# Opening order of TensorE's work, and the place of the w1 stage in the first and last block of a fused attention and MLP kernel

## The chip, the core and the metric

The kernel runs on one core of one Trainium2 chip. The metric is the device time of one execution in microseconds (us), as the median over several runs. The hardware profiler gives one more execution, with a trace of every instruction on TensorE (PE for products, PEld for weight loads), the vector engine (DVE), the scalar engine (ACT), GpSimd (POOL) and SyncE (SP), and of the DMA queues.

## What is computed

The input x has 2048 rows (tokens) of 576 columns. In outline, all in bfloat16:

```python
xn = layernorm(x)
# A: attention over the last W = 512 keys of a cache; 32 query heads, 16 key heads, head size 128
q  = xn @ wq                                  # 576 -> 32 * 128
p  = softmax(q @ k.T * 128 ** -0.5)           # no mask
s  = (p @ v) @ wo                             # 4096 -> 576
# B: a token-shift block and an MLP, on the same xn
h  = gelu(layernorm(xn) @ w1)                 # 576 -> 576
hs = (quarters of h shifted by +1, -1, +2, -2 rows) @ w2
x1 = xn + hs
b  = x1 + gelu(layernorm(x1) @ w3) @ w4       # 576 -> 4608 -> 576
out = x + s * silu(b)
```

## The kernel before

**Tiling.** The rows are cut into NB = 4 blocks of QB = 512, each of TB = 4 tiles of 128 rows. The first phase runs over blocks, and in each over the Hq = 32 heads. A step is one head of one block; its number is u = 32 * block + head, so there are 128 steps. The second phase (the MLP with w3 and w4, and the final combination) follows, block by block.

**One step of the first phase.** `stage_s(u, i)` makes four score tiles with keys as weights (L363), each followed by an exponential on ACT (L365). `stage_q(u + 1)` makes the next head's q with five 512-column products (L348). Its copy qT out of PSUM runs on the vector engine in block 0 (L353) and on ACT later (L355). `stage_v(u - 1, .)` makes the previous head's output in two halves of eight products (L380). The vector engine divides by the softmax sum (L384, L385) and writes a tile `o` from a ring of four buffers. `stage_t(u - 1)` sends a DMA transpose of `o` into `oT` on SP's queue (L393).

**Work put between.** Two dictionaries hold other work by step: `fill` (called once, after the next q) and `pe_fill` (lists of single products, cut in three and laid between the score tiles). The helpers `at`, `pe`, `spread` and `later` fill them. For each block they hold:
- `ln2_steps`: the LayerNorm for the w1 stage, at heads 7 to 9, and `tr2`: four DMA transposes on SP (L312) into `xnnT`, at heads 10 to 13
- `b1`: the w1 stage, five groups of five products (L452) on `xnnT`, with a GELU chain `gelu1_` on the vector engine and ACT after each group (L467 to L475), at heads 15 to 19
- `b2_shift`, `b2` and `b2_rem`: the w2 stage (L503) of the previous block, at heads 21 to 24, and in the last block also that of the last block itself, at heads 26 to 29; `b2_rem` ends with a 576 KB write of x1 to DRAM on SP's queue (L530)
- `wo_atoms`: the output product of the previous block, at heads 1 to 5
- `load_x` for the next block, `ln1_steps` (its LayerNorm, at heads 20 to 22 in block 0 and 24 to 26 in blocks 1 and 2) and `tr1` (its DMA transposes on SP's queue, L312, into `xT_b`, at heads 23 to 26 in block 0)
- `prep_k` (L247): four transposes on TensorE for one key head, with a copy out of PSUM, at the odd steps of block 0 up to 27

At the end of the last block come `load_x1(0)` at head 10, `ln3_steps(0)` from head 25 and `ln3_transpose(0)` at head 29 for the second phase.

**What sets the order.** `tc.manual_schedule(engines={SP, POOL, PE})` makes SP, POOL and TensorE run the first phase in the written order. The vector engine and ACT are ordered by a list scheduler, in which `tc.high_priority(offset=HP)` puts a section ahead of later work: the copies qT and kT, the division by the softmax sum, the GELU chain and the w2 additions have it, the LayerNorms don't. Each engine runs its list in order.

**Buffers.** The PSUM tiles are three for scores (tag `sc`), two shared by q, w1 and the remainder of w2 (`pq`), two for head outputs (`po`) and one (`wo`) shared by key transposes, wo and w2.

**The opening.** `ln1_steps(0)` is emitted first. TensorE then runs 32 small products of the identity with itself into `wu`, the key transposes of heads 0 and 1, four 512-column products of the identity with raw x, the 20 transposes of `tr1_first` (L319) into five PSUM tiles that ACT and the vector engine copy to `xT_b`, and the first q.

Of the kernel before, what the change touches and what calls it, by code (L numbers as in the profile page):

```python
# [8 lines left out]
P = 128  # L9
# [20 lines left out]
def kernel(  # L30
# [14 lines left out]
    nc = tc.nc  # L45
# [3 lines left out]
    _, S, D = A_x.shape  # L49
    _, Hkv, Sk, Dh = A_k_cache.shape  # L50
# [9 lines left out]
    QB = 512  # L60
    NB = S // QB
# [21 lines left out]
    ident = const.tile([P, P], BF16, name="ident")  # L83
# [88 lines left out]
    with ExitStack() as actx:  # L172
# [33 lines left out]
        x_t = {}  # L206
# [33 lines left out]
        def prep_k(g):  # L240
            st = {}
            src = kst_t[g // 4][:].rearrange("p a b -> p (a b)")[:, (g % 4) * W:(g % 4 + 1) * W]

            def tr(kc):
                if kc == 0:
                    st["ps"] = ps_wo.tile([P, W], BF16, name="ps_k", tag="wo")
                nc.tensor.transpose(out=st["ps"][:, kc * P:(kc + 1) * P], in_=src[:, kc * P:(kc + 1) * P],  # L247
                                    identity=ident[:, :])
                if kc == KCH - 1:
                    if g < 2:  # L250
                        nc.scalar.activation(out=kT[:, g, :], in_=st["ps"][:, :], func=ACT.Copy)
                        return
                    with tc.high_priority(offset=HP):
                        nc.vector.tensor_copy(out=kT[:, g, :], in_=st["ps"][:, :])

            return [lambda kc=kc: tr(kc) for kc in range(KCH)]

        def late(ap, fn):
            g = nc.gpsimd.tensor_copy(out=gate[:, :], in_=ap)
            with tc.issue_after(g.ins):  # L260
                fn()
# [44 lines left out]
        def ln1_steps(b):  # L306
            xn_t[b] = xn_b[b % 2]
            return layernorm_steps(small, [xn_b[b % 2][:, tt, 0:D] for tt in range(TB)], [x[:] for x in x_t.pop(b)],
                                   rsqrt_newton if b else rsqrt_table)
# [32 lines left out]
        def stage_q(u):  # L342
            qb, h = divmod(u, Hq)
            w = wq_b[(u // 4) % NWQ]
            hh = h % 4
            psq = ps_pq.tile([P, QB], FP32, name="psq", tag="pq")
            for kc in range(NDC):
                nc.tensor.matmul(psq[:, :], lhsT=w[:, kc, hh * Dh:(hh + 1) * Dh], rhs=xT_b[qb % 2][:, kc, :],  # L348
                                 start=(kc == 0), stop=(kc == NDC - 1))
            qT = qT_pool.tile([P, QB], BF16, name="qT")  # L350
            with tc.high_priority(offset=HP):
                if qb == 0:
                    nc.vector.tensor_copy(out=qT[:, :], in_=psq[:, :])  # L353
                else:
                    nc.scalar.activation(out=qT[:, :], in_=psq[:, :], func=ACT.Copy)  # L355
            qT_t[u] = qT
# [76 lines left out]
        def ln2_steps(b):  # L433
            return layernorm_steps(small, [xnn_b[:, tt, 0:D] for tt in range(TB)],
                                   [xn_t[b][:, tt, 0:D] for tt in range(TB)])

        def tr2(b, tt):
            transpose_tile(xnnT, xnn_b, tt)

        def b1(b, c):  # L440
            st = {}

            def mm(kc):
                if kc == 0:
                    if c == 0:
                        hb_t[b] = hb_pool.tile([P, 5, QB + 2 * PAD], BF16, name="hb")
                        if b == 0:
                            nc.vector.memset(hb_t[b][:, :, 0:PAD], 0.0)
                        if b == NB - 1:
                            nc.vector.memset(hb_t[b][:, :, PAD + QB:], 0.0)  # L450
                    st["ph"] = ps_pq.tile([P, QB], FP32, name="ph", tag="pq")
                nc.tensor.matmul(st["ph"][:, :], rhs=xnnT[:, kc, :],  # L452
                                 lhsT=w1r_sb[:, kc, :] if c == 4 else w1_sb[:, kc, c * c4:c * c4 + P],
                                 start=(kc == 0), stop=(kc == NDC - 1))
                if kc == NDC - 1:
                    gelu1(b, c, st["ph"])

            return [lambda kc=kc: mm(kc) for kc in range(NDC)]

        def gelu1(b, c, ph):  # L460
            with tc.high_priority(offset=HP):
                gelu1_(b, c, ph)
# [21 lines left out]
        def b2_shift(b):  # L484
            with tc.high_priority(offset=HP):
                b2_shift_(b)
# [67 lines left out]
        def at(u, fn):  # L554
            fill.setdefault(u, []).append(fn)

        def pe(u, atoms):
            pe_fill.setdefault(u, []).extend(atoms)
# [5 lines left out]
        def later(u, make, per):  # L564
            cell = []
            for i in range(2 * TB + 1):
                def step(i=i):
                    if not cell:
                        cell.append(make())
                    cell[0][i]()  # L570
                at(u + i // per, step)

        for b in range(NB):
            base = b * Hq
            if b > 0:
                for i, group in enumerate(wo_atoms(b - 1)):
                    pe(base + 1 + i, group)
            later(base + 7, lambda b=b: ln2_steps(b), 3)
            for tt in range(TB):
                at(base + 10 + tt, lambda b=b, tt=tt: tr2(b, tt))  # L580
            for c in range(5):
                pe(base + 15 + c, b1(b, c))
            for bb in ([b - 1] if b > 0 else []) + ([b] if b == NB - 1 else []):
                o2 = base + (26 if bb == b else 21)
                at(o2 - 1, lambda bb=bb: b2_shift(bb))
                for tt in range(TB):
                    pe(o2 + tt, b2(bb, tt))
                pe(o2 + 3, b2_rem(bb))
            if b + 1 < NB:
                at(base + (8 if b == 0 else 4), lambda b=b: late(pT_t[b * Hq + (8 if b == 0 else 4)][0][0:1, 0:1],  # L590
                                                                 lambda: load_x(b + 1, nc.gpsimd)))
                u1 = base + (24 if b else 20)
                later(u1, lambda b=b: ln1_steps(b + 1), 3)
                for tt in range(TB):
                    at(u1 + (3 + tt // 2 if b else 3 + tt), lambda b=b, tt=tt: tr1(b + 1, tt))
# [24 lines left out]
        at(3 * Hq + 4, finish_flag)  # L620

        with tc.manual_schedule(engines={SP, POOL, PE}):
            x_raw = x_t[0][0]
            for step in ln1_steps(0):
                step()
            wu = ps_sc.tile([P, QB], FP32, name="warm", tag="sc")
            for i in range(32):
                nc.tensor.matmul(wu[:, 0:P], lhsT=ident[:, :], rhs=ident[:, :], start=True, stop=True)
            for g in range(2):
                for fn in prep_k(g):  # L630
                    fn()
            for i in range(4):
                nc.tensor.matmul(wu[:, :], lhsT=ident[:, :], rhs=x_raw[:, 0:QB], start=True, stop=True)
            tr1_first()
            stage_q(0)
            for u in range(0, max(max(fill), max(pe_fill)) + 1):
                atoms = pe_fill.get(u, []) + [fn for v, g in pe_late if v == u for fn in prep_k(g)]
                n = len(atoms)
                cut = [atoms[0:n // 3], atoms[n // 3:2 * n // 3], atoms[2 * n // 3:]]
                for i in range(4):  # L640
                    if u < U:
                        stage_s(u, i)
                    if i == 0:
                        if u + 1 < U:
                            stage_q(u + 1)
                        for fn in fill.get(u, []):
                            fn()
                        continue
                    if i < 3 and 0 <= u - 1 < U:
                        stage_v(u - 1, 2 * (i - 1))  # L650
                    for fn in cut[i - 1]:
                        fn()
                if 0 <= u - 1 < U:
                    stage_t(u - 1)


    with ExitStack() as bctx:
# [90 lines left out]
        for b in range(NB):  # L748
# [20 lines left out]
            else:  # L769
# [9 lines left out]
                for i in range(3):  # L779
                    lo, hi = cuts[i], cuts[i + 1]  # L780
                    ps = pm[TB - 1 - i][:, 0:hi - lo]
                    for fc in range(FC):
                        nc.tensor.matmul(ps, lhsT=h3_t[fc][:, tt * P:(tt + 1) * P],
                                         rhs=w4_s[fc // WS][:, fc % WS, lo:hi], start=(fc == 0), stop=(fc == FC - 1))
# [4 lines left out]
    with tc.If(flag > 0):  # L789
        with ExitStack() as gctx:  # L790
# [19 lines left out]
            with tc.For_i(0, NT, 1) as t:  # L810
# [10 lines left out]
                for h in range(Hq):  # L821
                    g = h // REP
# [14 lines left out]
                    for kc in range(NDC):  # L837
                        nc.tensor.matmul(pq[:], lhsT=wq_sb[:, kc, h * Dh:(h + 1) * Dh], rhs=xnT[:, kc, :],
                                         start=(kc == 0), stop=(kc == NDC - 1))
# [19 lines left out]
                    for kc in range(KCH):  # L859
                        nc.tensor.matmul(po[:], lhsT=v_g[:, kc, :], rhs=pT[:, kc * P:(kc + 1) * P],  # L860
                                         start=(kc == 0), stop=(kc == KCH - 1))
# [5 lines left out]
                for ps, lo, hi in ((pm, 0, M0), (pr, M0, D)):  # L867
                    for h in range(Hq):
                        nc.tensor.matmul(ps[:], lhsT=oTs[h][:], rhs=wo_sb[:, h, lo:hi], start=(h == 0),
                                         stop=(h == Hq - 1))  # L870
# [39 lines left out]
```

## Time and profile before

| quantity | value |
|---|---|
| median of 12 runs | 870.26 us (865.8 to 882.49) |
| profiled execution | 867.96 us, of which the span in the trace is 865.9 us |
| TensorE products busy | 846.1 us (98% of the span) |
| ACT busy | 457.2 us (53%) |
| vector engine busy | 390.6 us (45%) |
| first score product starts | 16.07 us |
| last head output ends, first last-block wo product starts | 530.51 us |
| second phase, first w3 product starts | 561.9 us |

Times in the trace count from the start of the span. In lines of the trace, the first number is the start, the second the duration of the group, then engine, line, operation, tiles and shapes, and in brackets how long the engine had been idle and what released it. In lists of waits the three numbers are the total, how many times, and the longest. Matmuls are pipelined and their ends are modelled, so starts are the better numbers; the share of busy time is an average over stages.

### The profile page before, as it was taken

How to read it: one execution, taken by the hardware profiler on the slowest of the kernel's cores; microseconds unless marked ns; L12 is line 12 of the kernel's file. 1: busy time of each engine (PE TensorE's matmuls, PEld its weight loads, DVE VectorE, ACT ScalarE, POOL GpSimd, SP SyncE). 2: the span in 40 equal slices, each digit the busy share in tenths (PEclk: the TensorE clock that was granted, in tenths of full speed). 3: DMA queues.
4: the chain of work that ended last, by engine and by line, in shares of the span. 5: the costliest groups of instructions: out<-in, count | busy, mean ns of one | idle time of the engine just before them, and what ended most of it. 6: DMA issues, size and time to landing. Idle time of an engine off the chain costs nothing.

```text
span 865.9 us, 16302 instructions
## 1 busy us (share of the span) xinstructions
PE 846.1 (98%) x6512; PEld 472.6 (55%) x6512; DVE 390.6 (45%) x1210; ACT 457.2 (53%) x819; POOL 80.7 (9%) x143
## 2 busy tenths in 40 slices
PE   6989999999999999999999999999999999999996
PEld 4655655665665565565565565544444444444455
DVE  4778941278861287881155775000053026005024
ACT  4766763498783398784377873133242233225510
POOL 2432200310010110111010102000000000000000
PEclk9999999999999999999999999999999999999999
DMA  6995781374361184374147438990023005001001
GB/s 167 201 262 135 155 115 44 103 129 93 87 134 40 41 146 76 91 149 61 13 101 141 92 59 197 320 258 1 1 72 96 1 8 159 3 1 56 0 15 45
DMA packets 138098, 83.74 MB, mean 97 GB/s; under 512 B 104496, under 2 KB 131376, under 8 KB 138016
## 3 DMA queue, kind: packets, MB, share of 16 engines
q1 hardware_dynamic: 126448, 51.24, 30.1%
q0 software_dynamic: 8448, 28.15, 11.4%
q10 hardware_dynamic: 3120, 3.25, 1.1%
q8 instruction: 53, 0.87, 0.4%
q14 instruction: 29, 0.24, 0.1%
HBM read 49.17 MB, written 9.44 MB: 68 GB/s over the span
## 4 chain that ended last, share of the span: by engine, by line


## 5 line engine op out<-in xcount | busy, mean ns | idle before, releaser
L365 ACT ACTIVATE pT<-sc 128x512 bf16<-128x512 f32 x512 | 289.0, 596 | 107.0 <-PE sc L363 100.0
L363 PE MATMUL sc<-qT,kT 128*128 128x512 bf16 x512 | 182.6, 378 | 1.0 <-DVE qT L353 0.8
L705 PE MATMUL ph<-xT_b,w_s 128*128 128x512 bf16 x720 | 172.1, 379 | 0.0
L708 ACT ACTIVATE h<-ph 128x512 bf16<-128x512 f32 x144 | 85.6, 596 | 155.6 <-PE ph L705 151.0
L380 PEld LDWEIGHTS <-pT 128*128 128x128 bf16 x2048 | 139.2, 98 | 52.3 <-DVE o L385 1.8
L380 PE MATMUL po<-v_sb,pT 128*128 128x129 bf16 x2048 | 162.0, 220 | 0.4 <-ACT pT L365 0.4
L348 PE MATMUL psq<-xT_b,wq_b 128*128 128x512 bf16 x640 | 159.0, 379 | 0.5 <-DVE xT_b L325 0.3
L714 PE MATMUL pm<-w_s,h 128*128 128x512 bf16 x540 | 145.8, 380 | 0.0
L728 DVE TENSOR_TENSOR bs<-pm,x 128x512 f32<-128x512 f32 (+3 forms) x18 | 11.1, 629 | 246.3 <-PE pm L714 198.4
L404 PE MATMUL pswo<-wo_sb,oT 128*128 128x512 bf16 x512 | 116.5, 379 | 0.0
L384 DVE RECIPROCAL ri<-po 128x2 f32<-128x2 f32 x256 | 42.5, 166 | 162.6 <-PE po L380 159.4
L385 DVE TENSOR_TENSOR o<-po,ri 128x256 bf16<-128x256 f32 x256 | 107.6, 420 | 9.3 <-DMA oT<-o 3.1
L705 PEld LDWEIGHTS <-w_s 128*128 128x128 bf16 x720 | 63.8, 98 | 73.4
L348 PEld LDWEIGHTS <-wq_b 128*128 128x128 bf16 x640 | 62.4, 98 | 74.5 <-issue 2.4
L715 PE MATMUL pr<-w_s,h 128*128 128x64 bf16 x540 | 99.1, 193 | 0.0
L404 PEld LDWEIGHTS <-oT 128*128 128x128 bf16 x1024 | 64.9, 98 | 55.2
L714 PEld LDWEIGHTS <-h 128*128 128x128 bf16 x540 | 52.7, 98 | 63.8 <-issue 0.6
L355 ACT ACTIVATE qT<-psq 128x512 bf16<-128x512 f32 x96 | 57.4, 598 | 27.9 <-PE psq L348 27.9
L363 PEld LDWEIGHTS <-kT 128*128 128x128 bf16 x512 | 47.5, 97 | 29.4 <-DVE qT L353 1.3
L715 PEld LDWEIGHTS <-h 128*128 128x128 bf16 x540 | 51.0, 98 | 12.2 <-issue 0.4
L220 POOL DMA_DIRECT2D wq_b<-in_A_wq_dram x30 | 23.3, 778 | 310.3 <-PE psq L348 237.7
L414 ACT ACTIVATE s_out<-pswo 128x512 bf16<-128x512 f32 x16 | 9.6, 597 | 48.2 <-PE pswo L404 48.2
(101 smaller groups left out, 509.6 us busy)
## 6 DMA issues: line engine op xcount, KB each, us to landing
wq_b<-in_A_wq_dram POOLq DMA_DIRECT2D x30, 512.0 KB, 5.4
w_s<-in_B_w_dram SPq DMA_DIRECT2D x9, 576.0 KB, 8.8
wo_sb<-in_A_wo_dram POOLq DMA_DIRECT2D x8, 576.0 KB, 5.0
w_s<-in_B_w_dram SPq DMA_DIRECT2D x9, 512.0 KB, 9.5
x_dram<-x SPq DMA_DIRECT2D x4, 576.0 KB, 4.1
x<-x_dram SPq DMA_DIRECT2D x4, 576.0 KB, 4.5
s_b<-s_dram SPq DMA_DIRECT2D x4, 576.0 KB, 6.4
x_b<-in_A_x_dram SPq DMA_DIRECT2D x4, 576.0 KB, 6.1
```

What stands on the lines that cost most here:

```text
L348: nc.tensor.matmul(psq[:, :], lhsT=w[:, kc, hh * Dh:(hh + 1) * Dh], rhs=xT_b[qb % 2][:, kc, :], start=(kc == 0), stop=(kc == NDC - 1))
L355: nc.scalar.activation(out=qT[:, :], in_=psq[:, :], func=ACT.Copy)
L363: nc.tensor.matmul(sc[:, :], lhsT=kT[:, g, kc * P:(kc + 1) * P], rhs=qT_t[u][:, :], start=True, stop=True)
L365: nc.scalar.activation(out=pT[:, :], in_=sc[:, :], func=ACT.Exp, scale=SCALE)
L380: nc.tensor.matmul(po[:, j, :], lhsT=pTs[kc][:, tt * P:(tt + 1) * P], rhs=v_sb[:, g, kc, 0:Dh + 1], start=(kc == 0), stop=(kc == KCH - 1))
L384: nc.vector.reciprocal(out=ri[:], in_=po[:, :, Dh])
L385: nc.vector.tensor_tensor(out=o[:, t0:t0 + 2, :], in0=po[:, :, 0:Dh], in1=ri[:].unsqueeze(2).to_broadcast([P, 2, Dh]), op=ALU.mult)
L404: nc.tensor.matmul(ps, lhsT=oT_t[qb * Hq + h][:, tt, :], rhs=wo_sb[:, h, lo:hi], start=(h == 0), stop=(h == Hq - 1))
L705: nc.tensor.matmul(ph[:, :], lhsT=w3[:, kc, f0:f0 + P], rhs=xT_b[b % 2][:, kc, :], start=(kc == 0), stop=(kc == NDC - 1))
L708: nc.scalar.activation(out=h3[:, :], in_=ph[:, :], func=ACT.Gelu_apprx_tanh)
L714: nc.tensor.matmul(pm[tt][:, :], lhsT=lhsT, rhs=w4[:, fc % WS, 0:M0], start=(fc == 0), stop=(fc == FC - 1))
L715: nc.tensor.matmul(pr[:, tt, :], lhsT=lhsT, rhs=w4[:, fc % WS, M0:D], start=(fc == 0 and tt == 0), stop=(fc == FC - 1), skip_group_check=True)
```

## The change

In the opening, the 32 identity products become 36. The key transposes of head 0 follow, then 28 more identity products in place of the four 512-column ones, then `tr1_first` and the first q. The second key head's transposes move behind the first q. In blocks 0 and 3, the w1 stage goes from heads 15 to 19 to heads 17 to 21. In block 3 the w2 stage of block 2 goes from heads 21 to 24 to heads 23 to 26, and that of block 3 from heads 26 to 29 to heads 28 to 31. `b2_shift` moves along with each. Everything else is emitted at the steps where it was.

```diff
             for c in range(5):
-                pe(base + 15 + c, b1(b, c))
+                pe(base + (15 if 0 < b < NB - 1 else 17) + c, b1(b, c))
             for bb in ([b - 1] if b > 0 else []) + ([b] if b == NB - 1 else []):
-                o2 = base + (26 if bb == b else 21)
+                o2 = base + (28 if bb == b else 23 if b == NB - 1 else 21)
                 at(o2 - 1, lambda bb=bb: b2_shift(bb))
...
         with tc.manual_schedule(engines={SP, POOL, PE}):
-            x_raw = x_t[0][0]
             for step in ln1_steps(0):
                 step()
             wu = ps_sc.tile([P, QB], FP32, name="warm", tag="sc")
-            for i in range(32):
-                nc.tensor.matmul(wu[:, 0:P], lhsT=ident[:, :], rhs=ident[:, :], start=True, stop=True)
-            for g in range(2):
-                for fn in prep_k(g):
-                    fn()
-            for i in range(4):
-                nc.tensor.matmul(wu[:, :], lhsT=ident[:, :], rhs=x_raw[:, 0:QB], start=True, stop=True)
+
+            def warm(n):
+                for _ in range(n):
+                    nc.tensor.matmul(wu[:, 0:P], lhsT=ident[:, :], rhs=ident[:, :], start=True, stop=True)
+
+            warm(36)
+            for fn in prep_k(0):
+                fn()
+            warm(28)
             tr1_first()
             stage_q(0)
+            for fn in prep_k(1):
+                fn()
             for u in range(0, max(max(fill), max(pe_fill)) + 1):
```

## The prediction

> **What bounds the kernel now.** I read the page first: engine shares, then the list of TensorE's waits, then the timeline of the opening, of the two places where the w1 stage begins, and of what the vector engine and SP do after the first of them.
>
> ```profile
> PE 846.1 (98%) x6512; PEld 472.6 (55%) x6512; DVE 390.6 (45%) x1210; ACT 457.2 (53%) x819; POOL 80.7 (9%) x143
> ```
>
> TensorE's sequence sets the end; a microsecond in which it stands still is a microsecond of the total, unless a later wait gives it back. Its waits (in total, times, longest):
>
> ```profile
> PE ph L452 <- DMA xnnT<-xnn_b: 3.3, 2, 2.8
> PE ps_k L247 <- ACT kT L251: 2.6, 1, 2.6
> ...
> PE ps_k L247 <- DMA x<-in_A_k_cache_dram: 1.6, 1, 1.6
> PE ph L452 <- issue: 1.6, 1, 1.6
> ```
>
> All four are in what the change touches. The opening, on TensorE (start, duration, then idle before and releaser):
>
> ```profile
> 6.74 0.61 PE L247 MATMUL ps_k<-ident,x 128*128 128x128 bf16 x4 [1.56 <-DMA x<-in_A_k_cache_dram]
> 9.98 0.58 PE L247 MATMUL ps_k<-ident,x 128*128 128x128 bf16 x4 [2.64 <-ACT kT L251]
> 10.36 1.91 PE L633 MATMUL warm<-xt,ident 128*128 128x512 bf16 x4
> 12.07 1.63 PE L319 MATMUL ps_x<-ident,xn_b 128*128 128x128 bf16 x20
> 13.99 1.30 PE L348 MATMUL psq<-xT_b,wq_b 128*128 128x512 bf16 x5 [0.29 <-DVE xT_b L325]
> 16.07 0.38 PE L363 MATMUL sc<-qT,kT 128*128 128x512 bf16 x1 [0.78 <-DVE qT L353]
> ```
>
> The normalised x tile is complete at 8.18 + 1.45 = 9.63 us (vector engine, L139), but its transposes start at 12.07: the second head's keys wait 2.64 us for their one PSUM tile, then four 512-column products go first. The two w1 starts, in blocks 0 and 3:
>
> ```profile
> 65.17 0.81 PE L452 MATMUL ph<-xnnT,w_sb 128*128 128x512 bf16 x3 [2.75 <-DMA xnnT<-xnn_b]
> ...
> 467.56 0.38 PE L452 MATMUL ph<-xnnT,w_sb 128*128 128x512 bf16 x1 [1.56 <-issue]
> ```
>
> After block 0's w1 stage, the vector engine:
>
> ```profile
> 107.30 0.42 DVE L385 TENSOR_TENSOR o<-po,ri 128x256 bf16<-128x256 f32 x1
> ...
> 112.12 0.42 DVE L385 TENSOR_TENSOR o<-po,ri 128x256 bf16<-128x256 f32 x1 [1.76 <-DMA oT<-o]
> ```
>
> and SP's queue there:
>
> ```profile
> 101.10 1.21 SPq L312 DMA_TRANSPOSE xT_b<-xn_b  x1
> 102.36 1.26 SPq L393 DMA_TRANSPOSE oT<-o  x1
> 103.72 1.25 SPq L312 DMA_TRANSPOSE xT_b<-xn_b  x1
> 105.02 1.38 SPq L393 DMA_TRANSPOSE oT<-o  x1
> ```
>
> Outputs of later heads already wait here for transposes that stand behind those of block 1's x.
>
> **What the skill says.** "TensorE: Matmul & The Clock Gate", section "What's actually happening": the array runs at half clock until a window of about 3.4 us was busy, and the window is free-running, so the switch moves from run to run. The trace agrees on two rates: the four 512-column products from 10.36 to 12.07 are 0.43 us apart, those of a later q 0.216. Full speed appears only inside the 20 transposes after 12.07; the 3.6 us of small products from 1.59 did not bring it. The same page, section "Part 4: PE-mode transpose", holds that transposes do not count as busy in the same way; this trace cannot tell, since products and transposes share the window before the switch. "DMA: Bandwidth & Descriptors", section "Queues, rings and completion order": on each DMA engine descriptors of a queue are taken in ring order. The trace fits: the x transpose issued at 103.72 lands after 8.1 us, and the oT transpose behind it after 7.0, against a median of 3.5.
>
> **Opening.** Removed: four 512-column products (1.71 us, 10.36 to 12.07). Added: 4 + 28 small products. Moved: four key transposes of the second head, behind the first q. The first group rises to 36 x 0.107 = 3.9 us, ends at 5.4 and still waits for keys landing at 6.74: free. Keys of the first head to 7.2; then 28 x 0.107 = 3.0 us at half clock, to 10.2 (1.6 us at full clock). Then tr1_first, its data ready at 9.63. At half clock its 20 transposes take 2.1 us to 12.3 and the PSUM copies begin at 12.45 instead of 13.51: **-1.1 us**. If the clock switches by about 9.4 (the product stream is unbroken from 6.74), small products end at 9.8, the transposes take 1.2, and copies begin at 11.1: **-2.4**. If transposes do not count and the switch comes only after 16, q, scores and values run at half speed for some 6 us, +1 to +2. Weights do not stop it: wq's first pair, issued at 2.70 and 3.21, landed at 9.4 and 9.6. The moved key transposes (4 x 0.056 to 0.107) fit in the 0.78 us wait for the first qT, their copy on ACT before the first exponential; without that cover 0.4 us. I take -1.3, with -2.4 and +1.5 as ends. Nothing limits it later: TensorE is the bound right after.
>
> **Block 0.** A head takes 2.88 us on TensorE, 3.10 with key transposes, 1.08 more with five w1 products. Head 15 takes 7.09 instead of 4.18: 2.9 us. Two heads later, the w1 products start at about 67.5, while xnnT landed at 65.1: that wait goes. No product is added. But the 5 GELU chains (7 vector operations each, some 2.1 us of spacing) move with it from heads 15-19 to 17-21 and now overlap heads 20-22, in which block 1's LayerNorm is queued. From 67.4 to 104.2 the vector engine is busy 35.3 of 36.8 us: saturated. LayerNorm has the lower priority; when TensorE is a head ahead, one more head of vector work is in front (1.7 us by spacing: qT 0.6, twice a reciprocal 0.12 and a product 0.34, keys 0.33 every other head). So its first apply (100.65 now) does not come earlier, and I put it 0 to 4 us later. What waits for it: SP issues block 1's first x transpose (fixed in order at head 23), behind it stands the oT transpose of head 22, and head 26's output needs that buffer of a ring of four. Today it lands at 102.36 + 4.8 = 107.2, the output is at 107.30: **no margin**. TensorE itself bears about 1.5 us of this (the 1.76 us wait at 112.12 lengthened its head from 2.88 to only 3.08). So with the apply unmoved, 2.9 - 1.5 = 1.4 us is given back, leaving 1.5; for each microsecond that apply is later, one more goes. In its favour: the 576 KB wo and 512 KB wq loads (issued 101.68 and 103.60, five to seven us each), which crowd these transposes, now run some 3 us before them. I take **-1.2** net; ends -2.9 (nothing given back) and +2.5 (apply 4 us later).
>
> **Block 3.** Head 15: 5.68 instead of 3.96, 1.7 us, goes likewise (xnnT is there before 467.6; the stage now begins near 471). There is no next LayerNorm of x here and qT is copied on ACT, so the vector engine has room: 25.7 of 35.2 us busy. The w2 groups of blocks 2 and 3 move two heads as well; the last now fills heads 28 to 31. That covers the end of attention, where exponentials lag: a 0.35 us wait at 529.74 and 0.2 us in the product before. Another 0.4: **-2.1**. What moves with it on SP: the 576 KB write of x1 (L530) now stands just before the last two oT transposes. They are issued at about 1.6 us after attention's end, as today (531.13 and 532.4 against 530.51), landing 4.0 later; the wo products first need them 30 x 0.216 = 6.5 us after. Margin under 1 us: ends -2.4 and +2. LayerNorm for the MLP shares heads with the w2 additions; its result is needed at 561.9 and its transposes go out at 520.5, so it has room.
>
> **Sum.** -1.3 - 1.2 - 2.1 = -4.6 us. The profiled execution was 867.96 us (span 865.9 and 2.1 around it), so it would be 863.4. The median of the runs shown is 870.26, 2.3 above; with the same step, **865.7 us**. 0.5% is 4.35 us, about what a measurement here can tell from no change; my sum stands just beyond it.
>
> **Rivals.** (1) *Everything is kept*: the crowding is gone, outputs do not wait, the clock is up early: -2.4 - 2.9 - 2.1 = -7.4, 862.9 us. For it: four plain waits in the list; against: the margin of zero at 107.3. (2) *Block 0 gives all back*: saturated vector engine, apply 2 us later, opening at half clock: -1.1 + 0.5 - 2.1 = -2.7, 867.6 us. For it: 35.3 of 36.8. (3) *Slower: the SP queue in block 0 becomes the bound.* Apply 4 us later, and head 22's oT transpose takes 8.4 us instead of 4.8, as its neighbours did (8.1, 7.0): output of head 26 is 7.6 us late against today, plus 0.3 through what follows. From 4.9 us on (1.5 of margin, 1.3 and 2.1 elsewhere) it decides: -4.9 + 7.9 = +3.0, 873.3 us. (4) *The change misses its place*: if waits are set by something else that moves along (xnnT later because SP is busy), both w1 starts wait again and only the opening counts: 869 us; SP's issue of xnnT is ahead of the moved part, so I give this little.
>
> **How the numbers follow.** My forecast 0.46, (1) 0.20, (2) with (4) 0.22, (3) 0.12. The forecast's own range is 863.5 to 868, a little over half of it beyond 4.35 us. Faster by over 0.5%: 0.28 + 0.20 = 0.48; slower by over 0.5%, only the far part of (3) and an opening left at half clock: 0.10; within: 0.42. The range of 8 in 10 takes in (1), (2) and the near part of (3): 862.0 to 871.3.
>
> **What would show it.** Right: first score product at 13.7 to 15.0 instead of 16.07; no wait on xnnT; block 0 with an o<-oT wait of 2 us or more around head 26; attention's end with no 0.35 us wait. Wrong: transposes and first q at 0.43 us a product until beyond 16; block 1's first apply no later in heads than now; TensorE waiting for oT after attention.

## The result and the profile after

The changed kernel takes 865.28 us in the median of 12 runs (861.05 to 884.96), against 872.12 us for the kernel before (49 runs in all): a ratio of 0.9924, with an interval of 0.9897 to 0.9952. In a later set of runs it was 0.9918 (0.9887 to 0.9950). The forecast was 865.7. The profiled execution took 865.29 us, of which the span is 863.5. Some executions of any version are disturbed and left out of the ratios; two profiles below (of `e2_b0` and `f4_after_wo_ln1`) were of that kind and are not read.

The engines' shares, and TensorE's two longest waits from its list (in total, times, longest):

```profile
PE 848.5 (98%) x6540; PEld 475.6 (55%) x6540; DVE 390.6 (45%) x1210; ACT 457.6 (53%) x819; POOL 80.8 (9%) x143
```

```profile
PE po L380 <- DVE o L385: 2.1, 1, 2.1
PE psq L348 <- DMA xT_b<-xn_b: 2.0, 1, 2.0
```

The waits before the w1 stages of blocks 0 and 3 and both on keys have gone from the top. (Before, the list put the 1.56 us of block 3 down to "issue", but the last transpose into `xnnT` landed at 467.47 there and the products began at 467.56: it was a wait for `xnnT` too.) Two others stand there instead: head outputs that wait for the vector engine, and block 3's first q that waits for its transposed x. The opening on TensorE:

```profile
1.59 4.02 PE L629 MATMUL warm<-ident 128*128 128x128 bf16 x36 [1.59 <-POOL ident masks.py:199]
5.92 0.61 PE L247 MATMUL ps_k<-ident,x 128*128 128x128 bf16 x4 [0.31 <-DMA x<-in_A_k_cache_dram]
6.32 1.96 PE L629 MATMUL warm<-ident 128*128 128x128 bf16 x28
8.62 1.47 PE L319 MATMUL ps_x<-ident,xn_b 128*128 128x128 bf16 x20 [0.34 <-DVE xn_b L139]
10.38 1.31 PE L348 MATMUL psq<-xT_b,wq_b 128*128 128x512 bf16 x5 [0.29 <-DVE xT_b L325]
11.53 0.39 PE L247 MATMUL ps_k<-ident,x 128*128 128x128 bf16 x4
12.47 0.38 PE L363 MATMUL sc<-qT,kT 128*128 128x512 bf16 x1 [0.56 <-DVE qT L353]
```

The 28 products take 1.96 us, not 28 x 0.107 = 3.0: the clock rose inside them, for at 6.8 us the spacing of their starts goes from 0.107 to 0.056 us. Scores start at 12.47, not 16.07. The first w1 products of block 0 and of block 3, in the same timeline:

```profile
65.96 0.59 PE L452 MATMUL ph<-xnnT,w_sb 128*128 128x512 bf16 x2
...
471.25 0.38 PE L452 MATMUL ph<-xnnT,w_sb 128*128 128x512 bf16 x1
```

No bracket stands at their ends: no wait. Then the vector engine, where block 1's LayerNorm and the outputs meet:

```profile
97.94 0.43 DVE L139 TENSOR_SCALAR xn_b<-xt,ln_mv,nr_y 128x576 bf16<-128x576 bf16 x1
...
100.63 0.16 DVE L384 RECIPROCAL ri<-po 128x2 f32<-128x2 f32 x1
104.68 0.42 DVE L385 TENSOR_TENSOR o<-po,ri 128x256 bf16<-128x256 f32 x1 [3.89 <-DMA oT<-o]
```

SP's queue, with the output transposes queued between those of block 1's x:

```profile
98.40 1.20 SPq L312 DMA_TRANSPOSE xT_b<-xn_b  x1
99.65 1.32 SPq L393 DMA_TRANSPOSE oT<-o  x1
101.06 1.23 SPq L312 DMA_TRANSPOSE xT_b<-xn_b  x1
102.34 1.87 SPq L393 DMA_TRANSPOSE oT<-o  x1
```

The oT transpose issued at 99.65 lands 4.9 us later, at 104.59, and the vector engine, which needs that buffer for its next `o`, resumes at 104.68. TensorE there and at block 3's start, and the granted clock (columns: stretch, length, TensorE busy with its instructions, clock, share of the DMA engines, GB/s):

```profile
105.16 0.64 PE L380 MATMUL po<-v_sb,pT 128*128 128x129 bf16 x8 [2.12 <-DVE o L385]
...
107.64 2.02 PE L348 MATMUL psq<-xT_b,wq_b 128*128 128x512 bf16 x5
...
384.70 1.38 PE L348 MATMUL psq<-xT_b,wq_b 128*128 128x512 bf16 x5 [2.02 <-DMA xT_b<-xn_b]
```

```profile
103.00:105.00 2.00, 0.04 (x1) 1.00 0.72 149
105.00:107.00 2.00, 1.84 (x18) 0.70 0.49 94
107.00:109.00 2.00, 2.00 (x6) 0.50 0.69 135
...
386.00:388.00 2.00, 2.00 (x15) 0.50 1.13 139
```

After each of these waits the clock drops to half for about 3.4 us, which costs another 1.7: from about 105.8 to 109.2 and from 385.7 to 389.1 the products start at half the rate. The "busy" column hides it: the engine is at 2.00 of 2.00 while a q takes 2.02 us instead of 1.24.

The difference of the two profiled executions by stage, from the starts of products. Block 0 is counted from the second q, which starts right after the first score, the other blocks from their own first q:

| stage | before | after | difference | forecast |
|---|---|---|---|---|
| start to first score | 16.07 | 12.47 | -3.60 | -1.3 |
| block 0 | 100.89 | 101.48 | +0.59 | -1.2 |
| block 1 | 133.76 | 133.76 | 0 | 0 |
| block 2 | 135.73 | 136.77 | +1.04 | 0 |
| block 3, to its first wo product | 143.84 | 143.26 | -0.58 | -2.1 |
| second phase, to the last product | 328.38 | 328.38 | 0 | 0 |
| sum | | | -2.55 | -4.6 |

The medians are 6.8 us apart, more than the two profiles (2.67 us). The profiled execution of before, at 867.96, was a quick one among 49 with a median of 872.12; that of after is at its median. So more than half of the gain in the medians (4.2 of 6.8 us) is a difference that no pair of traces shows. One part of it may be the old opening: in e3 and f1 below, which have it, scores started at 16.70 and 17.35, later than the 16.07 of before.

### The profile page after: what moved, and what is told of

It is laid out like the page before. It is cut to its first block, busy times and chain, and to the rows that moved or that the text cites. A ratio compares the mean times of both kernels' runs of the same rounds, so it can differ in the third digit from the quotient of the medians.

```text
span 863.5 us, 16356 instructions
## 1 busy us (share of the span) xinstructions
PE 848.5 (98%) x6540; PEld 475.6 (55%) x6540; DVE 390.6 (45%) x1210; ACT 457.6 (53%) x819; POOL 80.8 (9%) x143
## 4 chain that ended last, share of the span: by engine, by line
```

## The experiments

Accounts to tell apart: (a) the parts need each other, since `xnnT` arrives late in block 0 however early TensorE gets there, and an earlier opening only lengthens that wait unless the w1 stage moves too; (b) the parts add up, each with its own gain; (c) the opening alone is the gain. Beside that: what of block 0's gain comes back at the ring of `o`.

The runs came in four sets, each with its own runs of before: the change; e1 to e4; f0 to f4; g1, e6, g3 and g4. Only the first and the third hold the change itself, so the other ratios are compared with it across sets. The stages are those of the table above, in us. The traces of e1, e3 and e4 lack some matmul records, so their stages are good to about 0.2 us.

| kernel | ratio, interval | first score | block 0 | block 2 | block 3 |
|---|---|---|---|---|---|
| before | 1 | 16.07 | 100.89 | 135.73 | 143.84 |
| the change | 0.9924 (0.9897-0.9952) | 12.47 | 101.48 | 136.77 | 143.26 |
| e1_open | 1.0029 (1.0001-1.0056) | 16.14 | 110.13 | 136.76 | 143.18 |
| e2_b0 | 0.9964 (0.9933-0.9994) | - | - | - | - |
| e3_b3 | 1.0019 (0.9980-1.0058) | 16.70 | 101.93 | 135.22 | 141.85 |
| e4_open_b3 | 0.9995 (0.9966-1.0025) | 12.52 | 107.76 | 137.26 | 141.85 |
| f0_after, the change again | 0.9918 (0.9887-0.9950) | 16.02 | 101.99 | 140.87 | 141.63 |
| f1_before_wo | 0.9937 (0.9910-0.9965) | 17.35 | 99.73 | 136.16 | 143.03 |
| f2_after_wo | 0.9881 (0.9836-0.9926) | 12.68 | 99.41 | 136.36 | 141.63 |
| f4_after_wo_ln1 | 0.9879 (0.9830-0.9929) | - | - | - | - |
| g1_keys_last | 0.9916 (0.9877-0.9955) | 12.89 | 99.50 | 140.72 | 141.64 |
| e6_ln1early | 0.9901 (0.9864-0.9937) | 13.62 | 97.26 | 137.74 | 141.63 |
| g3_open_b3_wo | 0.9918 (0.9884-0.9952) | 14.17 | 97.63 | 137.30 | 141.64 |
| g4_best | 0.9912 (0.9883-0.9941) | 12.98 | 104.33 | 136.21 | 141.63 |

Block 1 took 133.75 to 134.48 us in every one of these profiles.

### The parts by themselves

The opening alone, on the kernel before, with `warm` as in the change:

```diff
...
-            for g in range(2):
-                for fn in prep_k(g):
-                    fn()
-            for i in range(4):
-                nc.tensor.matmul(wu[:, :], lhsT=ident[:, :], rhs=x_raw[:, 0:QB], start=True, stop=True)
...
+            warm(36)
+            for fn in prep_k(0):
+                fn()
+            warm(28)
             tr1_first()
             stage_q(0)
+            for fn in prep_k(1):
+                fn()
```

> The opening alone, both w1 and w2 stages as before. Theory (opening and block 3 carry the gain, block 0 gives all back): -3.6 us by the profile after (first score product at 12.5 instead of 16.1), in the median -2.5 to -4. Rival (block 0 carries 2.9 in most runs and the profiled execution of after was an unlucky one): opening only -1.5 to -2.5. In the profile: half clock gone before 8 us, q(32) 3.6 earlier than before, the two waits on xnnT (2.75 and 1.56 us) still there.

Measured: 1.0029, no gain, so that neither of the two expectations held. From the list of TensorE's waits, and the timeline of the opening and of the w1 start:

```profile
PE ph L452 <- DMA xnnT<-xnn_b: 9.7, 1, 9.7
```

```profile
8.18 0.61 PE L247 MATMUL ps_k<-ident,x 128*128 128x128 bf16 x4 [2.57 <-DMA x<-in_A_k_cache_dram]
8.58 3.19 PE L629 MATMUL warm<-ident 128*128 128x128 bf16 x28
11.57 2.27 PE L319 MATMUL ps_x<-ident,xn_b 128*128 128x128 bf16 x20
...
72.15 1.44 PE L452 MATMUL ph<-xnnT,w_sb 128*128 128x512 bf16 x3 [9.66 <-DMA xnnT<-xnn_b]
```

Two things differ from the profile of the whole change. TensorE could go on with the keys only at 8.18, after it had stood still for 2.57 us, and all 28 products and the 20 transposes ran at half clock: scores started at 16.14, as before. And in block 0 the last transpose into `xnnT` took 12.1 us to land, so TensorE waited 9.66.

Block 0 alone, and block 3 alone:

```diff
-                pe(base + 15 + c, b1(b, c))
+                pe(base + (17 if b == 0 else 15) + c, b1(b, c))
```

> Only the w1 stage of block 0 two heads later; opening, block 3 as before. Theory: the 2.75 us wait goes and comes back as a wait of head outputs on the oT transposes around head 27, perhaps with half clock after it: -0.5 to +1.0 us. Rival: -2.5 us or more, no such wait over 1 us on TensorE.

```diff
-                pe(base + 15 + c, b1(b, c))
+                pe(base + (17 if b == NB - 1 else 15) + c, b1(b, c))
...
-                o2 = base + (26 if bb == b else 21)
+                o2 = base + (28 if bb == b else 23 if b == NB - 1 else 21)
```

> Only block 3: w1 two heads later, w2 stages two heads later. Both theories: -1.7 to -2.1 us, the 1.56 us wait gone and nothing in its place. If the write of x1 now ahead of the last oT transposes costs: a wait of the wo products after attention, 0 or slower.

Measured: block 0 alone 0.9964, a gain of 0.4% whose interval nearly touches 1. That is some 3 us (0.5 to 5.8), nearer the rival's size than the theory's; whether a wait of head outputs came in is not shown. Block 3 alone cannot be told from no change in the runs, but its stage in the profile is 141.85 against 143.84 us: -2.0. It is 141.6 to 141.9 in each profile of a kernel with this part except that of the change itself, where the half clock after 384.70 runs into it. Without this part the stage took 143.0 to 143.2 us in e1 and f1, where TensorE waited before w1 for 0.7 and 0.8 us and not for 1.56: there the part would save some 1.4 us. In e3 block 0's wait is the old one, 2.45 us, this time with the half clock behind it.

The opening and block 3 together, w1 in block 0 left where it was (the edit is against the changed kernel):

```diff
-                pe(base + (15 if 0 < b < NB - 1 else 17) + c, b1(b, c))
+                pe(base + (17 if b == NB - 1 else 15) + c, b1(b, c))
```

> Opening and block 3, block 0 as before. Theory: as fast as the whole change (-5 to -6.5 us against before). Rival: 2 to 3 us slower than the whole change (-3.5 to -4.5 us against before), since block 0's part is missing.

Measured: 0.9995, so that both expectations failed here too. The opening took its early course (scores at 12.52) and block 3 was 2 us shorter, yet nothing is left of it:

```profile
65.74 1.44 PE L452 MATMUL ph<-xnnT,w_sb 128*128 128x512 bf16 x3 [6.88 <-DMA xnnT<-xnn_b]
```

The w1 stage starts at 65.74; before the change it was 65.17. Everything the opening had gained was waited away there: the last transpose into `xnnT` landed at 65.6, as late as before (65.0), though it had been issued 2.8 us earlier. It isn't so in every execution. In the profile of the change it landed at 62.1, and w1 at its old place would have waited about 3.4 us by my estimate (2.75, less 3.0 for the landing, plus 3.6 for the opening). The parts do not add up: +0.3%, -0.4% and +0.2% alone, -0.05% for two of them, -0.8% for all three.

### What makes xnnT late

Eight loads of `wo`, 576 KB each, are issued at heads 4, 7, ... 25 of block 0, on GpSimd's queue. They move here to heads 16 to 23, behind the `xnnT` transposes, once in the kernel before and once in the changed one; the change is repeated beside them.

```diff
-            at(4 + 3 * i, lambda i=i: late(pT_t[4 + 3 * i][0][0:1, 0:1], lambda: load_wo(i)))
+            at(16 + i, lambda i=i: late(pT_t[16 + i][0][0:1, 0:1], lambda: load_wo(i)))
```

> The whole change again, beside the next three. Theory now (the parts need each other: the last transpose of xnnT in block 0 lands 7 to 18 us after its issue, set by bulk loads and not by TensorE's pace, so an earlier opening only lengthens the wait there unless w1 is later): -0.5 to -0.9% against before, as measured. Rival (the first comparison was luck and the parts' 0 to -0.4% add up): -0.2 to -0.4%.

> The kernel before, only the eight wo loads of block 0 moved from heads 4, 7, ... 25 to heads 16 to 23. Theory (wo loads crowd the xnnT transposes): last xnnT lands within 5 us of its issue instead of 7, TensorE's 2.75 us wait on it shrinks to under 1 us, median -2.5 to -5 us against before and fewer slow executions. Rival (landing is slow by the transposes themselves, or by wq, v and x loads): wait and median unchanged within 1 us.

> The whole change with the wo loads at heads 16 to 23. Theory: xnnT is there long before head 17 in every execution; what is left is the wait of head outputs on oT behind block 1's x transposes near head 27, which the earlier end of the wo loads shortens: 1 to 3 us faster than the whole change. Rival: the loads now crowd heads 20 to 27 and the output wait grows: equal or 1 to 3 us slower than the whole change.

Measured: the kernel before gains 0.6% from this alone (0.9937), and the changed one goes to 0.9881. On the same chip `f2` has a median of 862.6 us in six runs and the change 866.0: 3.4 us less (2.3 to 6.3 when the runs are resampled), so f2 beats both kernels. Of the four `xnnT` transposes of block 0, the time from issue to landing in the kernel before and then in f1:

```profile
DMA to landing us min/median/max: 4.4/5.5/6.9
```

```profile
DMA to landing us min/median/max: 2.8/3.9/5.5
```

In f1 block 0 no longer waits for `xnnT`; the loads' price is a wait for wq, which they now delay:

```profile
PE psq L348 <- DMA wq_b<-in_A_wq_dram: 2.1, 1, 2.1
PE ph L452 <- DMA xnnT<-xnn_b: 0.9, 1, 0.9
```

The 0.9 is at 331.37, in block 2. The same move in e4, the kernel in which block 0's w1 stage is not shifted:

> The opening and block 3 as in the change, block 0's w1 stage where it was before, and the eight loads of wo moved to heads 16 to 23 of block 0. Without that move of the loads the same kernel measured 0.9995. Theory (block 0's shift of w1 is worth only the margin that it gives against the crowding of the transposes by the loads of wo; with the crowding gone the margin is worth nothing): as fast as the whole change with moved loads, 0.987 to 0.989, with no wait for xnnT in block 0. Rival (the w1 stage itself is better placed two heads later, or the earlier opening runs into the transposes in any case): 0.991 to 0.996, with a wait for xnnT of 1 us or more near 65 us.

In the profile it did what was expected of it. The same summary for block 0, of e4 and then of g3:

```profile
DMA to landing us min/median/max: 5.5/7.3/10.2
```

```profile
DMA to landing us min/median/max: 3.5/4.2/5.3
```

and the stretch in which the last of them is under way, of e4 and then of g3 (after the length come the clock, the DMA engines' share, GB/s):

```profile
56.00:64.00 8.00, 0.94 1.26 214
```

```profile
56.00:64.00 8.00, 1.00 1.01 184
```

Block 0 took 97.63 us instead of 107.76, with no `xnnT` wait in it. "DMA: Bandwidth & Descriptors" of the Trainium skill, section "Issuing engines are not separate DMA queues", says that transfers issued by SP and by GpSimd run on the same 16 DMA engines and interleave; the trace agrees: with the loads on GpSimd's queue moved, the last of these transposes on SP's queue takes 4.1 us to land and not 10.2. The ratio of g3, though, is the rival's: 0.9918 is no better than the whole change's. Its 12 runs lie between 859.4 and 871.5 us, and the profiled one, at 862.77, is the second quickest. What the others meet is not known.

### The price at the ring of outputs

`e6` begins block 1's LayerNorm at head 12 instead of 20 (not 17, as its expectation has it) and issues the transposes of all its four tiles at heads 19 to 22 instead of 23 to 26; `f4` does the same on top of `f2`.

```diff
-                u1 = base + (24 if b else 20)
+                u1 = base + (24 if b else 12)
...
-                    at(u1 + (3 + tt // 2 if b else 3 + tt), lambda b=b, tt=tt: tr1(b + 1, tt))
+                    at(u1 + (3 + tt // 2 if b else 7 + tt), lambda b=b, tt=tt: tr1(b + 1, tt))
```

> The whole change, with block 1's layer norm begun from head 12 of block 0 and not from head 17, and the transposes of its first tile issued at heads 19 to 22. Theory (the 2.1 us for which TensorE waits near 105 us is VectorE held 3.9 us by an output transpose that queues on SP behind block 1's transposes): the wait goes, and so does the half clock of about 3 us after it: 2 to 4 us less than the whole change, 0.990 to 0.987 of the kernel before. Rival (what is late there is set by the queue's traffic as a whole, so another wait takes the place, such as xT of block 3 near 385 us or a load of wq): under 1 us less than the whole change.

> As the previous one, and block 1's LayerNorm from head 12 instead of 20, its transposes at heads 19 to 22. Theory: the vector engine does it in the slack of heads 12 to 16, SP is never held, the o<-oT wait of 3.9 us and TensorE's 2.1 us wait behind it go: another 2 to 4 us, in all -8 to -12 us against before. Rival (TensorE would be held elsewhere, at xT_b in block 2 or by half clock): under 1 us.

Measured: in e6 the wait near 105 us is gone, and with it the half clock: block 0 takes 97.26 us, 4.2 less than in the change. What is left on top of TensorE's list is the wait before block 3:

```profile
PE psq L348 <- DMA xT_b<-xn_b: 2.1, 1, 2.1
```

The five profiles with block 0's w1 stage shifted and this LayerNorm at its old place (the change, f0, f2, g1, g4) all have that wait, of 1.48 to 3.73 us. So it is shown that the place of this LayerNorm and its transposes makes it. The medians move by less: 0.9901, at the upper end of what was expected, and not to be told from the change's 0.9918 to 0.9924; with `wo` moved as well, 0.9879 against 0.9881, nothing, which is the rival's outcome.

### The opening's courses

`g1` puts both keys behind the first q, so that TensorE's first products never wait for a key; `g4` has this and, to keep the loads off wq as well, `wo` at heads 5, 6, 16, 18, ... 26.

```diff
-            warm(36)
-            for fn in prep_k(0):
-                fn()
-            warm(28)
+            warm(80)
             tr1_first()
             stage_q(0)
-            for fn in prep_k(1):
-                fn()
+            for g in range(2):
+                for fn in prep_k(g):
+                    fn()
```

> The whole change, but the opening issues 80 warm-up products, the first tile's transposes, the first q, and only then both heads' keys, so no key's arrival stands before the first tile. Theory (the opening takes one of two courses, by whether the first keys land before about 7.5 us or after 8; in the late course TensorE idles over 2 us after its first products and runs at half clock until about 15 us): here TensorE never idles before the first tile, the clock is full by about 7 us in every execution, the first score product starts at 12 to 13 us and not at 16, and the median is 0.5 to 1.5 us under the whole change's (866.0 on the last chip). Rival: the keys' transposes, one PSUM tile after the other behind q, hold the first scores until 14 us or later; then the median is the whole change's or up to 2 us above it.

> The whole change, with the keys last in the opening (80 warm-up products, first tile, first q, then both keys) and wo's loads at heads 5, 6, 16, 18, 20, 22, 24 and 26. Theory: the sum of the two gains, 9 to 12 us less than the kernel before (0.986 to 0.990), no wait for a load of wq near 104 us. Rival: loads of wo between heads 16 and 26 crowd block 1's transposes, the wait near 105 us grows to 4 us or more, and it is level with the whole change at 0.992.

The opening of g1:

```profile
1.59 5.90 PE L629 MATMUL warm<-ident 128*128 128x128 bf16 x80 [1.59 <-POOL ident masks.py:199]
8.69 1.47 PE L319 MATMUL ps_x<-ident,xn_b 128*128 128x128 bf16 x20 [1.20 <-DVE xn_b L139]
...
12.67 0.38 PE L247 MATMUL ps_k<-ident,x 128*128 128x128 bf16 x4 [0.69 <-ACT kT L251]
12.89 0.38 PE L363 MATMUL sc<-qT,kT 128*128 128x512 bf16 x1
```

Scores start at 12.89, and at 12.98 in g4. That is two executions; in the seven profiles with the change's own opening they start as follows, with the time at which the first key let TensorE go on and that at which the products begin to follow each other at full rate:

| profile | first key | full rate | first score |
|---|---|---|---|
| after | 5.92 | 6.8 | 12.47 |
| e4 | 6.90 | 5.0 | 12.52 |
| f2 | 7.12 | 5.4 to 7.1 | 12.68 |
| e6 | 6.44 | 10.0 | 13.62 |
| g3 | 6.66 | 11.0 | 14.17 |
| f0 | 8.07 | about 14 | 16.02 |
| e1 | 8.18 | about 14 | 16.14 |

The two latest are those with keys after 8.0, but among the other five the keys do not set the order: in e6 and g3 they came earlier than in e4 and f2, and scores started 0.9 us or more later. The first score goes with the clock: where that is at full rate before the first tile's transposes (from about 8.6), scores start at 12.5 to 12.7, and where it rises later they follow it. What sets the time of the rise is not shown. It is not fixed in g1 and g4 either, where TensorE waits for no key: full rate came at 4.3 and at 7.5, that is 2.7 and 5.9 us after the first product of an unbroken stream, both before the first tile.

The gain did not reach the median (866.05, 0.9916). In this execution block 2, which the change does not touch, cost 140.72 us, for its w1 stage waited for its own `xnnT`, with half clock after it (the second line is the wait near head 26 of block 0):

```profile
PE ph L452 <- DMA xnnT<-xnn_b: 3.1, 1, 3.1
PE po L380 <- DVE o L385: 1.7, 1, 1.7
```

For `g4` the rival held. No load of wq is waited for, but block 1's first transpose, issued while loads of `wo` and wq are under way, takes 6.9 us to land (5.8 in the change), the output's behind it 6.0 (4.9), and the outputs wait longer:

```profile
107.29 1.05 PE L380 MATMUL po<-v_sb,pT 128*128 128x129 bf16 x8 [3.73 <-DVE o L385]
```

Block 0 took 104.33 us, half clock included. Its nine runs lie within 864.6 to 868.0: steady, and no better than the change. That the moved loads are what delays these transposes fits the times, but was not tested by itself.

## Why the prediction was right, and where its steps were not

The median came out as forecast, through errors that cancel; that the number fits so well is luck. Starting from -4.6 us for the profiled execution: the opening gained 2.3 more, block 0 lost 1.8, block 2 lost 1.0 and block 3 lost 1.5, which gives -2.6. The 2.3 us then added for the distance from profile to median did not belong to the changed kernel.

- **Opening, the term of -1.3: mis-sized.** It was -3.6 in the profile, beyond the end given as the best (-2.4). That end took the clock to rise by 9.4; it rose at 6.8, inside the 28 products. The keys came at 5.92, where the prediction took 6.74 as given. Over the seven executions the term lies between -3.6 and +0.1 against the profile of before, with a clock that rises at 5 to 14 us; the profile of the change is the best of them. The second key's transposes cost nothing, as said: they lie inside the wait for the first `qT` (11.53, before the wait of 0.56).
- **"Nothing limits it later": wrong.** `e1` and `e4` show what does. The same step stands behind the pricing of block 0: "`xnnT` landed at 65.1" was taken as a fixed lateness of 2.75 us. The last transpose took 6.9 us to land before, 7.3 in the profile of the change, 10.2 in e4 and 12.1 in e1. So with block 0's shift that block costs 0.6 us more than in the profile of before, but 6.3 us less (107.76 to 101.48) than in e4, which has the earlier opening without it. In the medians the shift alone gained some 3 us (e2).
- **Block 0, what is given back: the place right, the price too low.** The wait for an oT buffer near head 26 was foretold with its chain: LayerNorm's first apply later (0.9 us later, counted from the first score, in a range of 0 to 4), SP's x transpose, the oT transpose behind it, the ring of four. It stalls the vector engine for 3.89 us and TensorE for 2.12, and counted from the first score the first output of head 26 is 1.0 us later than before. To that the half clock adds 1.7, which no step had: g1, with 1.69 us of this wait and no half clock, took 99.50, and f0, with 2.23 and the half clock, 101.99. Of those 2.49 us the wait is 0.54.
- **Block 3, -2.1: right against the profile of before.** -2.0 (e3) to -2.2 (f0). Of the 2.2, head 15 gave 1.7 and the end of attention the other 0.5 (forecast 0.4), though its one visible wait shrank only from 0.35 to 0.25 us. Against e1 and f1 the part is worth some 1.4. No wo product waited for `oT`. In the profile of the change the half clock after 384.70 hid most of it.
- **Block 2: not in the prediction.** Its wait for `xnnT` (0.58 us) went, but that for `xT_b` grew from 0.23 to 2.02 and set off the half clock counted in block 3. The transposes of block 3's x took up to 6.8 us to land, 5.5 before. With w1 at heads 15 to 19, block 2 costs between 135.2 and 140.9 us in the profiles above. Why it varies so is not known.

The forecast's case in which block 0 gives all back described block 0 (+0.5 forecast, +0.59 measured) and, by chance, the profile's sum (-2.7). The slower one, SP's queue as the bound, did not come: it needed the output of head 26 to be 4.9 us late, the opening's gain counted apart, and it was 1.0 us late. g4, in which TensorE waited 3.73 us there, shows that the place can cost more.

## What to carry to other kernels

A wait that ends with a DMA is not removed by getting there earlier, and its length in one profile is no constant: before pricing an earlier start, ask what arrives next, and whether it will come any earlier when it is asked for earlier. A stage that is moved later for the sake of one wait may be worth far more as a margin for other gains, which a test of each part by itself does not show. And price a wait on TensorE of over two microseconds with the half clock that may follow it.

## What was not expected of the hardware

- **The clock can drop after waits of 2 us.** In the profiles of before, the change and ten of the experiments, none of 11 waits of TensorE between 1.0 and 1.97 us within attention was followed by half clock, 5 of 9 between 2.02 and 2.75 were, and all four of 3.08 us or more. It lasted 3.4 us each time where it was followed through (after the waits that end at 105.16 and 384.70, and in f0 at 109.23), and cost 1.7. The Trainium skill's "TensorE: Matmul & The Clock Gate", section "Why this matters for your kernels", advises against idle gaps of over about 3 us; here 2.02 us was enough in some executions. That 2.12 us did it in the change and not in f1 fits the free-running window which the same page describes.
- **DMA transposes have no fixed duration.** Those into `xnnT` landed between 2.6 and 12.1 us after issue. In block 0 the last took 10.2 us in e4 and 4.1 in g3, which differ only in where the loads of `wo` stand.
- **The granted clock in the profile's windows reads 1.00 early in the opening**, where the products do not come at full rate. From 2 to 5 us it reads 1.00 in all of these profiles, while the 128-column products begin 0.107 us apart until 4.2 us or later and 0.056 at full rate. There only the spacing of the products tells.
